# Weight-form stores on GpSimd's queue, and attention of batches 2 and 3 at other steps

## The chip, the cores and the metric

The kernel runs on one core of one Trainium2 chip. The metric is the device time of one execution in microseconds (us). TensorE (PE) multiplies and transposes, ScalarE (ACT) and VectorE (DVE) work element by element and empty TensorE's accumulator banks, GpSimd (POOL) and SyncE (SP) issue data transfers; ScalarE and VectorE issue none here.

## What is computed

Attention between tokens and a small state, then two feed-forward blocks one after the other. Sizes: x is 4 batches x 8 heads x 512 tokens x 64, the state 4 x 8 x 32 x 64; both blocks take 2176 rows (4 x 512 of x and 4 x 32 of the state) of width 512, with an inner width of 2048.

```python
def _attn_ref(x, state):
    scores = scale * np.matmul(x, state.transpose(0, 1, 3, 2))      # softmax over the state
    xread = np.matmul(softmax(scores), state)
    scores2 = scale * np.matmul(state, x.transpose(0, 1, 3, 2))     # softmax over the tokens
    sread = np.matmul(softmax(scores2), x)
    return np.concatenate([xread, sread], axis=2)
def _moe_ref(x, w_in, w_out):
    h = x @ w_in
    return (h - np.tanh(h)) @ w_out
def _moe2_ref(x, w_in, w_out):
    h = x @ w_in
    return (h * np.tanh(softplus(h))) @ w_out
def reference(...):
    return _moe2_ref(_moe_ref(tokens of _attn_ref, w1i, w1o), w2i, w2o)
```

## The kernel before, in words

**Precision and weights.** The inputs' weights are 64-bit floats, read as pairs of 32-bit words. `conv_steps` makes a 32-bit float of each: ScalarE makes `w` and `r` from the two words of a stage buffer (`st`, or one of three tiles `wide`), VectorE joins them, and ScalarE's reading of the buffer lets `load_next` issue the next 512 KB load (lines L187 and L189) into it. Matmuls are three products each (`mm3p`): every operand is split into a large part (`wh`, `gh`, `ath`, `swh`, `yh`: a ScalarE copy) and a small one (`wl`, `gl`, `atl`, `swl`, `yl`: a VectorE subtraction).

**Two phases.** Phase 1 is attention and the first block; phase 2 is the second block, with seven products (`m1` to `m7`) where eight would be needed. In phase 1 a loop runs over `seq`: 16 steps for each of batches 0, 1 and 2, four for the state rows, 16 for batch 3 (`start` is 0, 16, 32, 48 and 52; the phase ends at 68). A step multiplies up (`up_x`: `h<-ath,swh`, where `sw` is `state @ w_in`, made by `sw` in groups of side products `swp` for each quarter of the inner width), applies `h - tanh(h)` (`t`, `gh`, `gl`), and three steps later multiplies down into four accumulators (`acc`, banks a0 to a3). At the end of a batch the accumulators are evicted to `y`, those of the state steps (bank a0 alone) to `ys`. The next batch's `acc` matmuls need these banks.

**Side work.** Two more banks, s0 and s1, serve all small products in turn (`side_bank`): `swp` takes both, then come `xtp` (x transposed), `sct` (scores), `sc` and `e2p` (transposed back), `srd` (the state's read) and `atp`. Each must be evicted before the one after the next can use its bank. `side` holds what runs at which step, written by `at`. With `back=1` the work is held behind marks of the step before on each engine; with `narrow` the mark on TensorE alone.

**Background pieces.** While phase 1 runs, `keep_pace` runs pieces of the conversion of the second block's weights: convert, add, split, store. `store_split` and `steps_2o` put the two halves of a form into `stores`; `send` issues those that are old enough, 256 KB each (line L257), to DRAM (`wi` and `wo`), and frees the slot in SBUF of a form when HOLD = 6 more pieces have run. 96 such stores are issued. Phase 2 loads the forms again (`ws`, L793; `wo`, L800). A slot that is used again by another tile must wait until the store that reads it has landed; the wait stands on the engine that writes the tile.

Every engine runs its instructions in one order that is fixed when the program is built, and so does each queue: an issue that waits holds back those behind it. SyncE issues all loads of weights, all stores and the reloads; GpSimd issues the eight loads of x for batches 2 and 3.

Of the kernel before, what the change touches and what calls it, by code (L numbers as in the profile page):

```python
# [25 lines left out]
MOST = 3  # L26
# [46 lines left out]
def attention_moe_kernel(  # L73
# [10 lines left out]
    nc = tc.nc  # L84
# [16 lines left out]
    TE, AC, V = (Pinned(e, order) for e in (nc.tensor, nc.scalar, nc.vector))  # L101
# [19 lines left out]
    def put(*units):  # L121
        for u in units:
            if u.slot is None:
                halves.append(u)
            else:
                free.append(u.slot)
# [119 lines left out]
    def run_piece():  # L246


        bg.popleft()()
        now[0] += 1  # L250
        send(now[0] - 1, now[0] - HOLD)

    def send(ready, gone):
        while stores and stores[0][0] < ready:
            _, u, d = stores.popleft()
            v = u.t.bitcast(F32)
            nc.sync.dma_start(  # L257
                out=d, in_=v if len(d.shape) == 2 else v.rearrange("p (g e) -> p g e", g=2)
            )
            sent.append((now[0], u))  # L260
        while sent and sent[0][0] < gone:
            put(sent.popleft()[1])
# [128 lines left out]
    def at_xt(b, k):  # L391
        xt_t(b, k)
        xt_c(b, k)
# [31 lines left out]
    def at_scores(b):  # L425
        sc_m(b)
        for j in range(2):
            sc_c(b, j)
# [26 lines left out]
    def at_exp(b, j):  # L455
        sc_t(b, j)
        sc_max(b, j)
        sc_sub(b, j)
        sc_exp(b, j)
# [19 lines left out]
    def at_norm(b, j):  # L479
        nm_sum(b, j)  # L480
        nm_rec(b, j)
        nm_mul(b, j)
# [54 lines left out]
    def at_steps(b):  # L537
        st = [lambda k=k: at_xt(b, k) for k in range(KD - 1)]
        return st + [
            lambda: at_xt(b, KD - 1),  # L540
            lambda: at_scores(b),
            lambda: (at_exp(b, 0), at_exp_t(b, 0)),
            lambda: at_norm(b, 0),
            lambda: (at_exp(b, 1), at_exp_t(b, 1), at_read_t(b, 0)),
            lambda: at_norm(b, 1),
            lambda: at_read_t(b, 1),
            lambda: at_sread(b),
        ]
# [454 lines left out]
    engines = (TE, AC, V)  # L1003
    marks = []

    def at(step, fn, back=None, narrow=False):

        def held():
            kept = [e.floor for e in engines]
            for e, m in zip(engines, marks[-back]):  # L1010
                if e is TE or not narrow:
                    e.floor = m
            fn()
            for e, m in zip(engines, kept):
                e.floor = m

        side.setdefault(step, []).append(held if back else fn)

    seq = []
    start = {}  # L1020
# [24 lines left out]
                at(k + 3, lambda b=b: at_sread(b), 1)  # L1045
    for b in (2, 3):
        at(start[b - 1], lambda b=b: load_x(b))
        for i, f in enumerate(at_steps(b)):
            at(start[b - 1] + 3 + i, f, 1, True)
    for b in (1, 2, 3):  # L1050
        at(start[b] - (3 if b > 1 else 1), lambda b=b: at_a(b))
    at(start[3], lambda: bg.extend(pieces_y(0) + list(late)))
# [3 lines left out]
    def keep_pace(i):  # L1056
        for (s0, n0), (s1, n1) in zip(pace, pace[1:]):
            if s0 <= i < s1:
                goal = n0 + (n1 - n0) * (i + 1 - s0) / (s1 - s0)
                ran = done[0]  # L1060
                for _ in range(MOST):
                    if done[0] < goal and bg and len(free) >= RESERVE:
                        run_piece()
                        done[0] += 1
                if ran == done[0]:
                    now[0] += 3
                    send(now[0], now[0] - HOLD)
# [120 lines left out]
    AC.last = pre  # L1188
    background(len(bg), 0)
    send(now[0] + 1, 0)  # L1190
    bg.extend(tail)
    for f in loads_in(0):
# [54 lines left out]
```

## Time and profile before

| what | value |
|---|---|
| time, median of 3 runs | 736.38 us (735.43 to 737.16) |
| the profiled execution | 737.36 us, of which 735.2 is the span from the first to the last instruction |
| TensorE busy | 711.4 us, 97% of the span |
| VectorE, ScalarE, GpSimd busy | 466.7, 353.3 and 6.6 us |
| SyncE's queue (hardware) | 115.89 MB |
| GpSimd's queue (software) | 2.10 MB |
| TensorE's granted clock, mean | 0.991 of full speed |

Busy times are of one execution under the profiler and lie between its first and last instruction; about 2 us are outside them. A matmul of the usual form (128x128 by 128x512) follows the one before at 0.227 us, so twelve take 2.72 us in the chain of work. The granted clock is a share of 2.4 GHz; 0.5 is the lower level, 1.2 GHz.

### The profile page before, as it was taken

Reading aid. Unit: us, or ns where it says so; the run is one execution under the profiler, and the core shown is the slowest. Engines: PE = TensorE matmul, PEld = TensorE weight load, DVE = VectorE, ACT = ScalarE, POOL = GpSimd, SP = SyncE. Lnnn points to the kernel's source line nnn. Section 1 sums busy time; section 2 is a strip of 40 time slices with the busy share of each in tenths; the row PEclk is TensorE's granted clock in tenths of the full one; section 3 lists DMA queues with packets and bytes.
Section 4 is the critical chain, followed back from the end, with each engine's and each line's share of the span. In section 5 each row is a group of like instructions: output and inputs, shape, how many; then the busy total and the mean of one; then the engine's idle time right before and its main releaser. Section 6 shows DMA issues by size and latency. Waiting matters only on the chain.

```text
span 735.2 us, 10518 instructions
## 1 busy us (share of the span) xinstructions
PE 711.4 (97%) x3968; PEld 568.2 (77%) x3968; DVE 466.7 (63%) x791; ACT 353.3 (48%) x631; POOL 6.6 (1%) x14
## 2 busy tenths in 40 slices
PE   8899999999899999699999999999999999999997
PEld 6467877788677898477877888888788888888886
DVE  5899654866657658766836776555753465445554
ACT  6998544565755567655636442333333333222320
POOL 0000010000000000000000000000000000000000
PEclk9999999999999999889999999999999999999999
DMA  9984120036842569600997725554676343422003
GB/s 298 339 296 141 58 57 1 1 115 209 289 132 88 201 203 292 247 3 6 313 363 259 257 90 185 172 173 128 235 238 224 119 157 115 150 94 71 1 1 129
DMA packets 66978, 118.65 MB, mean 161 GB/s; under 512 B 7280, under 2 KB 28016, under 8 KB 66928
## 3 DMA queue, kind: packets, MB, share of 16 engines
q1 hardware_dynamic: 66288, 115.89, 48.0%
q0 software_dynamic: 640, 2.10, 0.9%
q8 instruction: 31, 0.51, 0.3%
q14 instruction: 19, 0.16, 0.1%
HBM read 88.34 MB, written 29.62 MB: 160 GB/s over the span
## 4 chain that ended last, share of the span: by engine, by line
PE 77%; ACT 10%; DVE 5%; DMA 5%; issue 1%; SPq 1%; DVEq 0%; ACTq 0%
PE acc L60 42%; PE h L60 28%; ACT w L60 2%; DMA wi<-wh 2%; ACT r L60 2%; PE hs L60 2%; PE swp L60 1%; DVE wide L60 1%; ACT gh L60 1%; DVE gl L60 1%; PE srd L60 1%; ACT wide L60 1%; ACT wh L60 1%; DMA x<-in_x_dram 1%; ACT swh L60 1%
## 5 line engine op out<-in xcount | busy, mean ns | idle before, releaser
L60 PE MATMUL acc<-wo,gh 128*128 128x512 f32 x544 | 167.9, 390 | 0.3 <-ACT gh L60 0.3
L60 PE MATMUL h<-yh,ws 128*128 128x512 f32 x448 | 157.0, 392 | 1.8 <-DVE wide L60 1.8
L60 PEld LDWEIGHTS acc<-wo,gh 128*128 128x128 f32 x544 | 101.5, 188 | 21.5 <-ACT gh L60 0.8
L60 PE MATMUL acc<-gh,wh 128*128 128x512 f32 x244 | 100.9, 413 | 8.5 <-ACT ys L60 6.3
L60 PE MATMUL acc<-wo,gl 128*128 128x512 f32 x272 | 106.0, 390 | 0.0
L60 PEld LDWEIGHTS h<-yh,ws 128*128 128x128 f32 x448 | 84.1, 188 | 20.8 <-DVE wide L60 3.6
L60 DVE TENSOR_TENSOR wide<-acc,wide 128x512 f32<-128x512 f32 (+1 forms) x85 | 57.9, 683 | 63.0 <-PE acc L60 61.4
L60 PE MATMUL acc<-gh,wl 128*128 128x512 f32 x244 | 96.8, 397 | 0.0
L60 PE MATMUL acc<-gl,wh 128*128 128x512 f32 x244 | 96.8, 397 | 0.0
L60 DVE TENSOR_TENSOR wide<-h,wide 128x512 f32<-128x512 f32 x97 | 66.6, 687 | 33.4 <-ACT wide L60 18.2
L60 PE MATMUL h<-yl,ws 128*128 128x512 f32 x224 | 87.3, 390 | 0.0
L60 DVE TENSOR_TENSOR gl<-wide,gh 128x512 fp32r<-128x512 f32 x74 | 51.1, 690 | 39.7 <-ACT gh L60 38.1
L60 ACT ACTIVATE wide<-wide 128x512 f32<-128x512 f32 x47 | 29.7, 633 | 79.5 <-DVE wide L60 79.5
L60 PEld LDWEIGHTS acc<-gh,wh 128*128 128x128 f32 x244 | 46.7, 192 | 26.7 <-ACT ys L60 6.7
L60 ACT ACTIVATE wide<-h 128x512 f32<-128x512 f32 x43 | 25.5, 593 | 81.2 <-PE h L60 81.1
L60 PEld LDWEIGHTS acc<-wo,gl 128*128 128x128 f32 x272 | 51.1, 188 | 11.0 <-DVE gl L60 0.4
L60 PEld LDWEIGHTS acc<-gh,wl 128*128 128x128 f32 x244 | 46.7, 191 | 10.3
L60 PEld LDWEIGHTS acc<-gl,wh 128*128 128x128 f32 x244 | 46.9, 192 | 9.3 <-issue 0.8
L60 PE MATMUL h<-ath,swh 128*128 128x512 f32 x128 | 51.7, 404 | 1.8 <-DVE t L60 1.6
L60 ACT ACTIVATE gh<-wide 128x512 fp32r<-128x512 f32 x74 | 46.7, 632 | 11.1 <-DVE wide L60 9.3
L60 PE MATMUL h<-atl,swh 128*128 128x512 f32 x128 | 50.2, 392 | 0.0
L60 PE MATMUL h<-ath,swl 128*128 128x512 f32 x128 | 50.1, 391 | 0.2 <-DVE swl L60 0.2
(156 smaller groups left out, 957.8 us busy)
## 6 DMA issues: line engine op xcount, KB each, us to landing
ws<-wi SPq DMA_DIRECT2D x128, 256.0 KB, 3.8
wo<-wo SPq DMA_DIRECT2D x64, 256.0 KB, 3.7
st<-in_moe_w_in_dram SPq DMA_DIRECT2D x27, 512.0 KB, 5.5
st<-in_moe_w_out_dram SPq DMA_DIRECT2D x22, 512.0 KB, 5.0
wi<-wh SPq DMA_DIRECT2D x32, 256.0 KB, 4.0
wi<-wl SPq DMA_DIRECT2D x32, 256.0 KB, 4.0
wide<-in_moe_w_out_dram SPq DMA_DIRECT2D x10, 512.0 KB, 5.2
wo<-wh SPq DMA_DIRECT2D x16, 256.0 KB, 3.8
```

Source lines behind the costliest of these rows:

```text
L60: i = fn(*args, **kw)
```

## The change

Three parts. (1) `send` issues the stores of weight forms on GpSimd's queue in place of SyncE's. (2) The eleven steps of attention of batches 2 and 3 stand at other distances from the batch's start, 3, 4, 5, 7 and so on to 15 in place of 3 to 13, and TensorE's part of them is no longer held behind the mark of the step before; the groups of `state @ w_in` stand at distances 2, 6, 10 and 14. (3) From step 58 on, `keep_pace` may run four pieces in a step in place of three. No instruction of TensorE, ScalarE or VectorE is added or taken away.

```diff
--- before.py
+++ after.py
@@ -254,7 +254,7 @@
         while stores and stores[0][0] < ready:
             _, u, d = stores.popleft()
             v = u.t.bitcast(F32)
-            nc.sync.dma_start(
+            nc.gpsimd.dma_start(
                 out=d, in_=v if len(d.shape) == 2 else v.rearrange("p (g e) -> p g e", g=2)
             )
             sent.append((now[0], u))
@@ -1003,13 +1003,12 @@
     engines = (TE, AC, V)
     marks = []
 
-    def at(step, fn, back=None, narrow=False):
+    def at(step, fn, back=None):
 
         def held():
             kept = [e.floor for e in engines]
             for e, m in zip(engines, marks[-back]):
-                if e is TE or not narrow:
-                    e.floor = m
+                e.floor = m
             fn()
             for e, m in zip(engines, kept):
                 e.floor = m
@@ -1045,8 +1044,8 @@
                 at(k + 3, lambda b=b: at_sread(b), 1)
     for b in (2, 3):
         at(start[b - 1], lambda b=b: load_x(b))
-        for i, f in enumerate(at_steps(b)):
-            at(start[b - 1] + 3 + i, f, 1, True)
+        for i, f in zip((3, 4, 5, 7, 8, 9, 10, 11, 12, 13, 15), at_steps(b), strict=True):
+            at(start[b - 1] + i, f)
     for b in (1, 2, 3):
         at(start[b] - (3 if b > 1 else 1), lambda b=b: at_a(b))
     at(start[3], lambda: bg.extend(pieces_y(0) + list(late)))
@@ -1058,7 +1057,7 @@
             if s0 <= i < s1:
                 goal = n0 + (n1 - n0) * (i + 1 - s0) / (s1 - s0)
                 ran = done[0]
-                for _ in range(MOST):
+                for _ in range(MOST + (i >= start[3] + 6)):
                     if done[0] < goal and bg and len(free) >= RESERVE:
                         run_piece()
                         done[0] += 1
```

The order of the program shows what moves. The first place is ScalarE's queue ahead of `ys`, the eviction of the state's accumulator; `t` and `gh` belong to the main path, `swh` to the next side products, `w`, `r`, `wh` and `yh` to the background pieces, and a wait on DMAHW or DMASW is one for a transfer of SyncE's or GpSimd's queue. Before:

```order
L60 ACTIVATE wh_3294<-w_3239 128x512 [waits PE_49]
L60 ACTIVATE yh_3512<-y_2190 128x512 [waits DMAHW4_49]
L60 ACTIVATE t_3255<-h_3248 128x512 [waits PE_49]
L60 ACTIVATE w_3341<-st_2925 128x512 [waits DMAHW3_49,PE_49]
L60 ACTIVATE swh_3276<-swp_3263 128x512 [waits DMAHW5_49,PE_49]
L60 ACTIVATE r_3342<-st_2925 128x512
L60 ACTIVATE gh_3258<-t_3255 128x512 [waits DMAHW1_49,DVE_49]
L60 ACTIVATE swh_3272<-swp_3262 128x512 [waits PE_49]
L60 ACTIVATE yh_3552<-yt_3354 128x512 [waits DMAHW1_49]
L60 ACTIVATE wh_3350<-w_3341 128x512 [waits DVE_49,PE_49]
L60 ACTIVATE ys_3292<-acc0_3126 128x512 [waits PE_49]
```

After:

```order
L60 ACTIVATE t_3166<-h_3159 128x512 [waits DMASW7_49,DMASW0_49,PE_49]
L60 ACTIVATE gh_3169<-t_3166 128x512 [waits DVE_49]
L60 ACTIVATE wh_3253<-w_3185 128x512 [waits PE_49]
L60 ACTIVATE r_3306<-st_2946 128x512 [waits DMAHW6_49,DVE_49]
L60 ACTIVATE t_3214<-h_3207 128x512 [waits PE_49]
L60 ACTIVATE wh_3299<-s34_3202 128x512 [waits PE_49]
L60 ACTIVATE swh_3235<-swp_3222 128x512 [waits PE_49]
L60 ACTIVATE gh_3217<-t_3214 128x512 [waits DVE_49]
L60 ACTIVATE swh_3231<-swp_3221 128x512 [waits DMASW6_49,PE_49]
L60 ACTIVATE yh_3470<-wide_73 128x512 [waits DMASW4_49]
L60 ACTIVATE ys_3251<-acc0_3085 128x512 [waits PE_49]
```

Of the ten items ahead of `ys` five waited for a transfer before (the two `yh`, `w`, a `swh` and `gh`) and four do after; behind the state's last `gh`, three items stood ahead of `ys`, and now two do.

The second place is SyncE's queue at the end of batch 1: loads (`st`) and stores (`wi`, `wo`) of weight forms. Before:

```order
L189 DMA st_2002<-in_moe2_w_in_dram 128x1024 [waits DMAHW0_49,Activation_49]
L189 DMA st_2010<-in_moe2_w_in_dram 128x1024 [waits DMAHW1_49,Activation_49]
L189 DMA st_2102<-in_moe2_w_in_dram 128x1024 [waits DMAHW3_49,DMAHW2_49,Activation_49]
L257 DMA wi_86<-wh_2092 128x2x256
L257 DMA wi_86<-wl_2093 128x2x256 [waits DMAHW4_49,DVE_49]
L257 DMA wo_111<-wh_2133 128x512 [waits DMAHW5_49]
L257 DMA wo_111<-wl_2134 128x512 [waits DMAHW6_49,DVE_49]
L257 DMA wo_112<-wh_2146 128x512 [waits DMAHW7_49]
L257 DMA wo_112<-wl_2147 128x512 [waits DMAHW0_49,DVE_49]
L189 DMA st_2141<-in_moe2_w_in_dram 128x1024 [waits DMAHW1_49,Activation_49]
```

After, SyncE's queue and GpSimd's at the same place:

```order
L189 DMA st_2029<-in_moe2_w_in_dram 128x1024 [waits DMAHW7_49,Activation_49]
L189 DMA st_2037<-in_moe2_w_in_dram 128x1024 [waits DMAHW1_49,Activation_49]
L189 DMA st_2129<-in_moe2_w_in_dram 128x1024 [waits DMAHW0_49,Activation_49]
L189 DMA st_2228<-in_moe2_w_in_dram 128x1024 [waits DMAHW2_49,Activation_49]
L189 DMA st_2272<-in_moe2_w_out_dram 128x1024 [waits DMAHW3_49,Activation_49]
```

```order
L257 DMA wi_86<-wh_2121 128x2x256 [waits DMASW6_49,Activation_49]
L257 DMA wi_86<-wl_2122 128x2x256 [waits DMASW7_49,DVE_49]
L257 DMA wo_111<-wh_2221 128x512 [waits DMASW0_49,Activation_49]
L257 DMA wo_111<-wl_2222 128x512 [waits DMASW1_49,DVE_49]
L257 DMA wo_112<-wh_2233 128x512 [waits DMASW2_49,Activation_49]
L257 DMA wo_112<-wl_2234 128x512 [waits DMASW3_49,DVE_49]
L257 DMA wo_113<-wh_2277 128x512 [waits DMASW4_49,Activation_49]
L257 DMA wo_113<-wl_2278 128x512 [waits DMASW5_49,DVE_49]
```

The loads now follow one another with no store between, and the stores stand behind stores.

The third place is ScalarE's queue ahead of `y`, the eviction of batch 1's accumulators. Before:

```order
L60 ACTIVATE t_2157<-h_2150 128x512 [waits PE_49]
L60 ACTIVATE swh_2178<-swp_2165 128x512 [waits DMASW3_49,PE_49]
L60 ACTIVATE gh_2160<-t_2157 128x512 [waits DVE_49]
L60 ACTIVATE swh_2174<-swp_2164 128x512 [waits PE_49]
L60 ACTIVATE w_2307<-st_2010 128x512 [waits DMAHW3_49,DMAHW1_49]
L60 ACTIVATE y_2185<-acc0_1307 128x512 [waits PE_49]
L60 ACTIVATE r_2308<-st_2010 128x512 [waits DMAHW4_49]
L60 ACTIVATE y_2195<-acc2_1309 128x512 [waits PE_49]
```

After:

```order
L60 ACTIVATE wide_72<-h_2134 128x512 [waits PE_49,Activation_49]
L60 ACTIVATE swh_2161<-swp_2148 128x512 [waits DMASW0_49,PE_49]
L60 ACTIVATE gh_2143<-wide_72 128x512 [waits DVE_49]
L60 ACTIVATE swh_2157<-swp_2147 128x512 [waits PE_49]
L60 ACTIVATE w_2281<-st_1747 128x512 [waits DMAHW1_49,DMASW0_49]
L60 ACTIVATE wide_72<-acc0_1307 128x512 [waits DVE_49,PE_49]
L60 ACTIVATE y_2177<-acc2_1309 128x512 [waits PE_49]
```

The first eviction of an accumulator stood behind a `w` that waits for two transfers of SyncE's queue; it now stands behind a `w` that waits for one of each queue. (The tile of the first eviction has another name because a slot of `wide` serves it.)

The fourth place is TensorE's queue behind the side products for batch 2's second group. Before, one transpose follows the last `swp` behind nine `acc` matmuls:

```order
L60 MATMUL swp_2361<-w_545,sbt_76 32x512
L60 MATMUL acc0_2225<-gh_2214,wh_541 128x512
L60 MATMUL acc0_2225<-gl_2215,wh_541 128x512
L60 MATMUL acc0_2225<-gh_2214,wl_542 128x512
L60 MATMUL acc1_2226<-gh_2214,wh_541 128x512
L60 MATMUL acc1_2226<-gl_2215,wh_541 128x512
L60 MATMUL acc1_2226<-gh_2214,wl_542 128x512
L60 MATMUL acc2_2227<-gh_2214,wh_541 128x512
L60 MATMUL acc2_2227<-gl_2215,wh_541 128x512
L60 MATMUL acc2_2227<-gh_2214,wl_542 128x512
L60 MATMUL xtp_2379<-ident_75,x_2072 128x128 [waits DMASW4_49,DVE_49]
```

After, it stands behind all twelve and the six of `h`:

```order
L60 MATMUL acc2_2207<-gh_2194,wl_542 128x512
L60 MATMUL acc3_2208<-gh_2194,wh_541 128x512
L60 MATMUL acc3_2208<-gl_2195,wh_541 128x512
L60 MATMUL acc3_2208<-gh_2194,wl_542 128x512
L60 MATMUL h_2373<-ath_1860,swh_2157 128x512 [waits DVE_49]
L60 MATMUL h_2373<-atl_1862,swh_2157 128x512
L60 MATMUL h_2373<-ath_1860,swl_2158 128x512
L60 MATMUL h_2373<-ath_1869,swh_2161 128x512
L60 MATMUL h_2373<-atl_1871,swh_2161 128x512
L60 MATMUL h_2373<-ath_1869,swl_2162 128x512
L60 MATMUL xtp_2387<-ident_75,x_2060 128x128 [waits DMASW6_49,DVE_49]
```

The transposes moved nine matmuls further from the group whose banks they use.

## Rows read from the trace of the kernel before

**Rows 1.** The page, busy time, share and instructions of each engine
```profile
PE 711.4 (97%) x3968; PEld 568.2 (77%) x3968; DVE 466.7 (63%) x791; ACT 353.3 (48%) x631; POOL 6.6 (1%) x14
```

**Rows 2.** What TensorE waited for: releaser, us in total, times, longest
```profile
PE acc L60 <- ACT ys L60: 6.3, 1, 6.3
...
PE acc L60 <- ACT y L60: 2.2, 1, 2.2
```

**Rows 3.** The chain of work, 300 to 319 us: start, us, what
```profile
310.43 5.49 PE acc L60 x12
315.92 1.78 PE h L60 x6
```

**Rows 4.** Timeline of TensorE, 300 to 320: start, us, instruction, idle before
```profile
310.43 0.80 PE L60 MATMUL acc<-gh,wh 128*128 128x512 f32 x1 [6.28 <-ACT ys L60]
```

**Rows 5.** Timeline of ScalarE, 296 to 312 us
```profile
305.14 0.63 ACT L60 ACTIVATE yh<-y 128x512 fp32r<-128x512 f32 x1 [2.05 <-DMA wo<-wh]
...
309.77 0.60 ACT L60 ACTIVATE ys<-acc 128x512 f32<-128x512 f32 x1
```

**Rows 6.** Stretches: us, busy time of each engine, granted clock, DMA share, GB/s
```profile
180.00:200.00 20.00, 17.27 (x83) 12.87 (x82) 13.71 (x23) 14.36 (x27) 1.44 (x2) 0.93 0.91 307
...
303.50:318.00 14.50, 8.22 (x26) 6.18 (x25) 10.51 (x17) 7.76 (x15) 0.00 (x0) 0.65 0.45 165
```

**Rows 7.** The chain of work, 196 to 206 us
```profile
190.35 6.09 DMA wi<-wh
...
197.73 4.35 PE acc L60 x12
```

**Rows 8.** Timeline of SyncE's queue, 181 to 197 us
```profile
186.05 4.26 SPq L189 DMA_DIRECT2D st<-in_moe_w_in_dram  x3
```

**Rows 9.** The chain of work, 206 to 240 us
```profile
220.04 2.95 PE acc L60 x12
...
228.91 2.72 PE acc L60 x12
231.63 1.36 PE h L60 x6
```

**Rows 10.** The stores' line: durations ns min/median/max, first and last start, waits, landing
```profile
L257 SPq DMA_DIRECT2D wi<-wh x32: 359/374/1419, 160.0 to 367.5; - x32
...
L257 SPq DMA_DIRECT2D wo<-wl x16: 319/320/1180, 192.0 to 411.2; - x16
...
  ACT yh L60: 4.7, 2
  ACT w L60: 4.6, 2
...
DMA to landing us min/median/max: 2.1/3.9/6.5
```

**Rows 11.** The loads' line: issues on GpSimd, duration ns min/median/max, first and last start
```profile
L363 POOL DMA_DIRECT2D x<-in_x_dram x6: 722/722/838, 90.8 to 164.9; - x6
```

**Rows 12.** The page, DMA issues: count, KB each, median us to landing
```profile
st<-in_moe_w_out_dram SPq DMA_DIRECT2D x22, 512.0 KB, 5.0
...
x<-in_x_dram POOLq DMA_DIRECT2D x6, 256.0 KB, 3.2
...
wide<-in_x_dram POOLq DMA_DIRECT2D x2, 256.0 KB, 5.5
```

**Rows 13.** Timeline of TensorE, transposes that waited, 190 to 240 us
```profile
194.83 0.66 PE L60 MATMUL xtp<-ident,wide 128*128 128x128 f32 x4 [0.48 <-DVE swl L60]
...
216.28 0.66 PE L60 MATMUL xtp<-ident,x 128*128 128x128 f32 x4 [0.39 <-DVE swl L60]
...
235.53 0.65 PE L60 MATMUL e2p<-ident,scs 128*128 128x128 f32 x4 [0.63 <-DVE swl L60]
```

**Rows 14.** Timeline of ScalarE, 255 to 297 us
```profile
282.78 0.60 ACT L60 ACTIVATE wide<-acc 128x512 f32<-128x512 f32 x1
```

**Rows 15.** Timeline of TensorE, 281 to 290 us
```profile
286.31 0.48 PE L60 MATMUL acc<-wh,gh 128*128 128x512 f32 x1
```


## The prediction

> **What bounds the kernel now.** I read the page first. TensorE is busy for nearly the whole span [rows 1], so the kernel is bound by TensorE and only its own gaps and slow stretches can be won back; VectorE's and ScalarE's idle time is worth nothing by itself. Second came the list of what TensorE waited for. One wait stands far above the rest, for `ys`, the eviction of the finished state accumulator, and the next that this change can touch is that for `y`, the eviction of batch 1 [rows 2]. Then I followed both through the chain of work and ScalarE's timeline.
>
> The state wait: TensorE stands still for 6.28 us and goes on at 310.43 [rows 4]. ScalarE is free before that, but stands 2.05 us in front of a split `yh` whose slot is freed by the landing of a `wo` store, and then has nine items queued ahead of `ys`, which starts at 309.77 [rows 5]. The granted clock of the stretch that holds this gap is 0.65, a mix of the two levels, 2.4 and 1.2 GHz [rows 6]. So the twelve `acc` matmuls behind the wait take 5.49 us and the six `h` matmuls 1.78 us [rows 3], where twelve and six take 2.72 and 1.36 elsewhere [rows 9].
>
> The `y` wait: SyncE's queue holds loads and stores in one order. At 186.05 three loads take it 4.26 us [rows 8], the store behind them is issued at 190.35 and lands 6.09 us later, and only then may ScalarE write a `w` that stands ahead of `y` [rows 7]. The twelve matmuls behind take 4.35 us [rows 7], where behind a set of small side products they take 2.95 [rows 9].
>
> In all, ScalarE waited for landings of stores in four places, 4.7 us at `yh` and 4.6 us at `w` [rows 10].
>
> **Part 1, stores on GpSimd's queue.** 96 issues leave SyncE; GpSimd, which has 8 loads, gets them. GpSimd computes nothing in this stretch. An issue on SyncE took 0.374 us in the middle [rows 10], one on GpSimd 0.722 [rows 11], so 96 issues are about 69 us of an engine that idles: no cost by itself. What changes is the order: a store no longer stands behind a load that waits for a stage buffer, and no load stands behind a store. Landing on SyncE's queue was 2.1 to 6.5 us, 3.9 in the middle [rows 10]; GpSimd's loads of the same size took 3.2 and, in the crowded stretch, 5.5 [rows 12].
>
> *The state wait.* After the change one item with a store ahead of it is left before `ys`, a `yh`, and its store (`wi_96<-wl_3254`) has its data 2.9 to 4.5 us before the state accumulator is done, an estimate from the matmuls that lie between in the order, at the pace of rows 9. From there: issue 0.72, landing 3.2 or 5.5, so 3.9 or 6.2 us; then two ScalarE items of about 0.5 us; and six `h` matmuls (1.36 us) that TensorE still has. With 3.2 the stall is 0 to 0.7 us, with 5.5 it is 1.4 to 3.0. Traffic there is light (165 GB/s against 307 in the transition, [rows 6]), so I take the quiet landing and 0.3 us. Gain: 6.28 for the wait, 5.49 - 2.72 = 2.77 and 1.78 - 1.36 = 0.42 for the clock, 9.47 us; left over, 0.3.
>
> *The transition from batch 1 to 2.* The stores leave the loads' queue, and no store behind loads holds the `w` ahead of `y` any more; a 512 KB load may. That load is issued only when the buffer has been read, six ScalarE items earlier, about one step of TensorE (12 + 6 matmuls, 4.08 us, [rows 9]) and its side products; a load of this size lands in 5.0 us [rows 12]. Gain: 2.2 for `y` [rows 2], 0.48 at the transposes just before [rows 13], which came late for the same backlog, and 4.35 - 2.95 = 1.40 for the clock: 4.1 us. I leave 0.3 (bounds 0 and 1.7, the latter if the load lands 1.4 us later than that).
>
> **Part 2, attention of batches 2 and 3 at other steps.** Nothing is added or removed; the transposes go where no group of `state @ w_in` products has just taken both side banks. Two waits behind such a group go: at 216.28 (0.39) and 235.53 (0.63) [rows 13], since at the first the next transposes stand 18 matmuls behind the group and no longer 9: 1.02 us. Two waits of the same kind further ahead, in batch 1, stay: there a transpose still stands within some nine matmuls of the group. Four new places appear, where a product or transpose follows the one before it by only 0 to 2 matmuls and needs a bank that ScalarE or VectorE must first evict. No row shows these; the nearest are the waits just named, 0.39 to 0.63 each, and none has a second eviction ahead of it as those had, so 0 to 0.45 each; I take 0.9 for the four (bounds 0 and 2.5).
>
> **Part 3, four pieces in place of three from step 58.** Conversions run a little earlier near the end of the phase. After the state stretch TensorE has slack in front of every reload of forms, and the order of MoE2 is as before, so I take nothing. Its cost, if the cover is gone, would be ScalarE items ahead of `h` evictions, 0.5 us each.
>
> **A cost that the new order brings.** Between batch 2 and the state steps ScalarE must evict accumulator 0 before the state sums start. Before, that ran at 282.78 [rows 14], some 0.6 us long, and TensorE wanted it at 286.31 [rows 15]: 2.9 us to spare. After, four conversions in a row stand ahead of it, each needing a 512 KB load that is issued only when the buffer before it is read. Worked through with load landings of 4 to 5.5 us (5.0 in the middle, [rows 12]), ScalarE comes out 0 to 3 us late. I take 1.0, near the lower end because the loads no longer stand behind stores.
>
> **Sum.** Gains 9.47 + 4.1 + 1.02 = 14.6; costs 0.3 + 0.3 + 0.9 + 1.0 = 2.5; net -12.1 us. The profiled execution took 737.36, 0.98 above the median shown, 736.38. So 725.3 for such an execution, **724.3** as a median. 0.2% is 1.5 us, about what a measurement of this kernel can tell from no change.
>
> **Rivals.**
> - *A: the wait comes back in another place.* `yh` before `ys` waits for a store that lands in 5.5 us, or the load chain ahead of accumulator 0 is 3 us late, and the clock falls again. For: GpSimd's two crowded loads took 5.5 [rows 12], and 2.2 us of standing still were followed by slow matmuls [rows 7]. Against: the state stretch is quiet. Price: 2.7 us more of stall and 3.2 of clock (2.77 + 0.42): 730.2; with one of the two alone 727 to 730, with both places hit 733.5 (2.0 more of stall and 1.3 of clock).
> - *B: the queue changes nothing but who issues.* Landing, not order, made the waits: 6.09 us of landing against 4.26 in SyncE's queue [rows 7, 8]. Then both big stalls stay, part 2 gives 1.0 - 0.9, and the time is 735 to 738, 736.3 in the middle. Against: `w` could have been written 4 us earlier with the store issued on time, and nine items no longer stand ahead of `ys`. The Trainium skill (DMA: Bandwidth & Descriptors, "Issuing engines are not separate DMA queues") says that transfers of all issuing engines share the same 16 DMA engines and that issuing from several saves only issue time. By that rule 736.3; the trace shows 4.26 us of such issue time at 186.05 [rows 8], more than the rule calls usual.
> - *C: slower, GpSimd's queue becomes the bound.* Stores ran from 160.0 to 411.2 us [rows 10], 96 of them, 2.6 us apart on average. If an issue on GpSimd took longer than that, the queue would fall behind, slots would come free late, and the splits that need them, then `ys` and the reloads, would wait. MoE2's reloads have some 14 us of slack (an estimate from the order, at the pace of rows 9), so the forecast's 12 us are gone when the lag is 26 us, at 2.9 us an issue (0.27 x 96); at 3.0 us it lags 38, and the time is 724.3 + 38 - 14 = 748. Against: all 6 loads of the row took 0.72 to 0.84 [rows 11], and two more 0.72 while VectorE was busy 13.7 of 20 us [rows 6]. The Trainium skill (SBUF — State Buffer, "A bandwidth-pool intuition that's wrong (but worth ruling out)") states that a transfer issued by GpSimd takes about 620 ns alone and about 3100 beside a VectorE copy, since its descriptors can't be written meanwhile. By that figure the lag is 48 us and the time 758; the eight loads here don't show it.
>
> **How the numbers follow.** Chances: forecast (721 to 727) 0.60, A 0.24, B 0.06, C 0.10. Lower end: costs at their lower bounds, 724.3 - 2.5 = 721.8, and 1 us of spread between runs, so 720.8. Upper end: A with both places hit, 733.5. That leaves out B, C and little else, under 2 in 10. The likeliest case's own range is 721 to 727.5. Faster by over 0.2%: forecast and A, 0.84. Within 0.2%: B, 0.06. Slower: C, 0.10.
>
> **What will show it.** Right: no TensorE wait for `ys` over 1 us; the granted clock at 1.0 from 196 to 206 and from 290 to 305 (the stretch moves forward by some 5 us); GpSimd with 104 issues of 0.7 us; SyncE's loads issued without a store between; waits for e2p, xtp, sct, atp of about 0.5 us each in number, not in size. Wrong: an `acc` wait of 2 us or more at the state sums with `yh` or `w` ahead of it, or clock below 0.9 there; an issue on GpSimd of over 2 us; `ws` reloads that TensorE waits for. The step I trust least is the landing of stores from GpSimd, since the trace has loads from there only.

## The result and the profile after

| | before | changed |
|---|---|---|
| median, 4 runs each, us | 736.77 (735.43 to 738.65; the three of the first table and one more) | **728.22** (726.63 to 729.65) |
| ratio | | 0.9882, 95% [0.985, 0.9913] |
| profiled execution, us (span) | 737.36 (735.2) | 726.63 (724.9) |

Changed is faster by 8.5 us in the median and by 10.7 us between the two profiled executions. The profiled execution of the changed kernel was its fastest, and the only one of the four with a mean granted clock of 1.000 (the others 0.995 to 0.998); that matters below.

The page of the changed kernel first: the row of the engines, then three rows of DMA issues (count, KB each, median us from issue to landing). They answer to [rows 1] and [rows 12].

```profile
PE 708.0 (98%) x3968; PEld 566.0 (78%) x3968; DVE 464.3 (64%) x791; ACT 352.9 (49%) x631; POOL 70.4 (10%) x110
...
st<-in_moe_w_in_dram SPq DMA_DIRECT2D x27, 512.0 KB, 5.9
...
wi<-wh POOLq DMA_DIRECT2D x32, 256.0 KB, 4.5
...
wo<-wh POOLq DMA_DIRECT2D x16, 256.0 KB, 5.4
```

TensorE has the same 3968 matmuls. GpSimd's busy time is now that of issuing, and the stores did not land in the 3.2 us of the quiet `x` loads.

What TensorE waited for (us in total, times, longest), against [rows 2]:

```profile
PE acc L60 <- ACT ys L60: 1.7, 1, 1.7
...
PE acc L60 <- ACT wide L60: 0.4, 1, 0.4
PE e2p L60 <- DVE swl L60: 0.4, 1, 0.4
```

The `ys` wait went from 6.3 to 1.7, the wait for `y` (whose first eviction is now named `wide`) from 2.2 to 0.4, and the side banks cost 0.4 at the dearest of the new places. The chain of waits at the state sums (start, duration), against [rows 3]:

```profile
299.15 2.82 DMA wi<-wl
301.99 0.03 ACT yh L60
...
302.53 0.59 ACT ys L60
...
303.16 3.06 PE acc L60 x12
306.22 1.36 PE h L60 x6
```

A `yh` waits for a store of `wl` to land, `ys` follows, and TensorE goes on at 303.16. This is the one item that the prediction said would be left ahead of `ys`. Here the clock held, and the twelve and six matmuls took 3.06 and 1.36 us, against 5.49 and 1.78. The windows show the clock (last three columns: granted clock, DMA share, GB/s):

```profile
180.00:200.00 20.00, 19.58 (x100) 15.06 (x99) 14.12 (x25) 13.47 (x25) 8.36 (x12) 1.00 0.69 237
...
300.00:312.00 12.00, 10.35 (x48) 8.20 (x47) 10.64 (x18) 9.87 (x19) 5.33 (x9) 1.00 0.82 256
```

Both are at 1.00, where [rows 6] had 0.93 and 0.65. The DMA engines are not quiet at the state sums any more: 256 GB/s, where the window of [rows 6] that holds the gap moved 165. While the store above was under way, from 299.15 to 301.97 us, the rate was 232.

**Where the time came from.** From step 21 on, every step of the main path but the state's four has six `h` matmuls, and the start of the first of them marks the step in TensorE's timeline. The mark of step 36, the first behind the eviction of `y`, stood at 201.91 before and stands at 199.54 now; that of step 57 stood at 320.75 and stands at 310.63. Differences between such marks split the gain by stretch (us, changed less before, profiled executions; "stores alone" and "steps alone" are the first two experiments):

| stretch | forecast | changed | stores alone | steps alone |
|---|---|---|---|---|
| start to step 21 | 0 | +0.7 | +2.2 | +1.6 |
| 21 to 35 (new side-bank waits) | +0.9 | +0.8 | 0.0 | +0.7 |
| 35 to 36 (transition, `y`) | -3.8 | **-3.8** | **+3.8** | -4.6 |
| 36 to 48 (old side-bank waits) | -1.0 | -0.3 | 0.0 | -1.3 |
| 48 to 55 (batch 2 to the state) | +1.0 | 0.0 | +1.8 | 0.0 |
| 55 to 57 (state sums, `ys`) | -9.2 | **-7.5** | -1.3 | **-8.7** |

The first line lies before the first store (156.3 us); over all the kernels run here it lies between -0.2 and +3.3 us, and nothing is read from it. In the fourth line a new wait of TensorE stands beside the old ones that went, for `xt` (x transposed, evicted by ScalarE) at about 211 us: 0.4 us in the changed kernel, none in e2, but 1.0 and 1.8 us in two other runs with the same steps (e12 and e6 below). The two places of the forecast gave the gain, in nearly the forecast sizes. Which part of the change gave it is another matter.

### The profile page after: what moved, and what is told of

Same layout as the page of the kernel before. It is cut to its first block, busy times and chain, and to the rows that moved or that the text cites. A ratio compares the mean times of both kernels' runs of the same rounds, so it can differ in the third digit from the quotient of the medians.

```text
span 724.9 us, 10570 instructions
## 1 busy us (share of the span) xinstructions
PE 708.0 (98%) x3968; PEld 566.0 (78%) x3968; DVE 464.3 (64%) x791; ACT 352.9 (49%) x631; POOL 70.4 (10%) x110
## 4 chain that ended last, share of the span: by engine, by line
PE 72%; issue 12%; ACT 6%; POOL 4%; DVE 4%; DMA 1%; SPq 0%; POOLq 0%; DVEq 0%; ACTq 0%
PE acc L60 39%; PE h L60 26%; POOL wi L257 3%; ACT w L60 2%; ACT r L60 2%; PE hs L60 2%; PE swp L60 1%; POOL wo L257 1%; PE srd L60 1%; DMA x<-in_x_dram 1%; DVE gl L60 1%; ACT gh L60 1%; DVE wide L60 1%; ACT t L60 1%; ACT swh L60 1%
## 5 line engine op out<-in xcount | busy, mean ns | idle before, releaser
L60 PE MATMUL acc<-gh,wh 128*128 128x512 f32 x244 | 99.3, 407 | 2.1 <-ACT ys L60 1.7
```

Of the source, the lines that this page charges most:

```text
L60: i = fn(*args, **kw)
```

## The experiments

**1 and 2: each part alone.** e1 has only the queue changed, e2 only the steps and pieces (stores on SyncE, as before).

```diff
 # e1_stores_only, in send
-            nc.sync.dma_start(
+            nc.gpsimd.dma_start(
 # e2_steps_only, where the steps are placed (and the at() and keep_pace of the change)
-        for i, f in enumerate(at_steps(b)):
-            at(start[b - 1] + 3 + i, f, 1, True)
+        for i, f in zip((3, 4, 5, 7, 8, 9, 10, 11, 12, 13, 15), at_steps(b), strict=True):
+            at(start[b - 1] + i, f)
```

> Part 1 alone: stores of weight forms on GpSimd's queue, attention steps and pieces per step as before. My account (the stores' place in SyncE's queue made the transition's wait, and the item order on ScalarE the state wait): the transition's gain of 3.8 us comes here, the state wait does not, since the store that held it was issued at once and landed in 2.5 us; TensorE's wait for ys stays at 5 to 7 us, and the time is 732.5 to 734. Rival (the queue makes both gains): wait for ys below 2.5 us and 726 to 729. Rival (the queue gives nothing): both waits as before, 735.5 to 737.5.

> Parts 2 and 3 alone: new attention steps and four pieces from step 58, stores on SyncE's queue as before. My account: the order on ScalarE ahead of ys is nearly that of the full change, so most of the state gain of 7.5 us comes, and the y wait of the transition stays at 2 us or more: 729 to 732. Rival (the queue makes both gains): the wait for ys stays above 4 us and the time is 735 to 738.

Measured: e1 741.65 us, ratio 1.0071 [1.0047, 1.0095]: **slower**, by 4.8 us against the 736.89 of the kernel before run beside it. e2 724.52, ratio 0.9847 [0.982, 0.9875]: faster by 12.4. Both lie outside every range that was written down for them. All that was gained came from the steps, and the queue, to which the prediction gave 13.6 of its 14.6 us of gains, costs time. TensorE's waits in e1:

```profile
PE xtp L60 <- DVE swl L60: 7.0, 3, 6.1
PE acc L60 <- ACT ys L60: 5.0, 1, 5.0
```

`ys` is 5.0 us late on GpSimd's queue too, and the transition is worse than before. ScalarE's timeline shows why (start, duration; in brackets idle time before it and what ended that):

```profile
189.57 1.21 ACT L60 ACTIVATE w<-st 128x512 f32<-128x512 f32 x2 [1.59 <-DMA wi<-wh]
...
194.59 0.66 ACT L60 ACTIVATE r<-st 128x512 uint32<-128x512 uint32 x1 [1.70 <-DMA st<-in_moe_w_in_dram]
...
198.03 0.66 ACT L60 ACTIVATE w<-st 128x512 f32<-128x512 f32 x1 [2.26 <-DMA st<-in_moe_w_in_dram]
198.60 0.64 ACT L60 ACTIVATE r<-st 128x512 uint32<-128x512 uint32 x1
199.14 0.58 ACT L60 ACTIVATE t<-h 128x512 f32<-128x512 f32 x1
199.62 0.59 ACT L60 ACTIVATE swh<-swp 128x512 fp32r<-128x512 f32 x1
```

A store wait is still there (1.59), and two conversions then wait 1.70 and 2.26 us for 512 KB loads, with `t` and `swh` of the main path queued behind them. That place in the queue is new too: in the kernel before, the same `w` stands behind `t` and both `swh`, right ahead of `y` (third place of the change section). So the edit of the queue alone also changed ScalarE's order here, and the 4.8 us hold both. The loads were not freed by the removal of the stores from their queue: SyncE's timeline has four of them spread over 12 us, although each is issued in 0.33, since in the program's order each waits for the ScalarE item that reads its buffer free.

```profile
187.48 12.12 SPq L189 DMA_DIRECT2D st<-in_moe_w_in_dram  x4
```

The store that held this `w` before did go out sooner. It is the `wi<-wh` that SyncE issued at 190.35 and that landed at 196.44 [rows 7]; in e1 GpSimd issues it at 185.38, and it lands after 6.1 us again, at 191.49:

```profile
185.38 0.73 POOL L257 DMA_DIRECT2D wi<-wh  x1
```

But the load of the same `w`, there at 192.15 before, now came at 197.95. The three loads of this place landed in 4.8 to 5.8 us before and in 7.0 to 9.3 in e1 (line L189, us from issue to landing, least, middle and most; before, from 186 to 192 us, then e1, from 187 to 193):

```profile
DMA to landing us min/median/max: 4.8/5.0/5.8
```

```profile
DMA to landing us min/median/max: 7.0/7.1/9.3
```

And the stretch is full. The window of e1 has the DMA engines busy 0.97 of it, and the stores issued from 176 to 196 us landed in 6.6 us in the middle (6.1 before):

```profile
180.00:200.00 20.00, 16.53 (x84) 12.42 (x82) 11.90 (x22) 13.01 (x24) 10.13 (x16) 1.00 0.97 336
...
DMA to landing us min/median/max: 4.1/6.6/8.1
```

In e2 nothing is wrong at the state sums: `yh` has no idle time ahead of it, and TensorE waits 0.5 us for `ys`.

```profile
298.87 0.63 ACT L60 ACTIVATE gh<-t 128x512 fp32r<-128x512 f32 x1
299.39 0.60 ACT L60 ACTIVATE swh<-swp 128x512 fp32r<-128x512 f32 x1
299.86 0.65 ACT L60 ACTIVATE yh<-wide 128x512 fp32r<-128x512 f32 x1
300.39 0.60 ACT L60 ACTIVATE ys<-acc 128x512 f32<-128x512 f32 x1
```

**3: which of the two parts that move no DMA.** e6 takes the fourth piece out of e2, and e3 takes it out of the changed kernel:

```diff
-                for _ in range(MOST + (i >= start[3] + 6)):
+                for _ in range(MOST):
```

> Part 2 alone: new attention steps, stores on SyncE's queue, three pieces in a step to the end. If part 3 is worth nothing, as forecast: 724 to 725.5, as parts 2 and 3 together (724.5). Rival (the fourth piece matters once the stores are on SyncE's queue, since five fewer pieces are done when phase 1 ends): 726 to 728, with waits of TensorE behind 350 us.

> The changed kernel without part 3: three pieces in a step to the end. My account, that part 3 is worth nothing: 727.5 to 729, as the changed kernel. Rival (the fourth piece brings the end of phase 1 forward or delays evictions): 1 us or more off in either direction, with new waits of TensorE between 310 and 360 us.

Measured: e6 725.37, ratio 0.9844 [0.9819, 0.987]; e3 727.1, ratio 0.9879 [0.9849, 0.9909]. They stand where e2 and the changed kernel stand, so the fourth piece is worth nothing that can be measured, and part 2 alone is worth some 12 us.

**4: which batch's steps.** The new distances for one of the two batches, the other at 3 to 13, stores on SyncE (e9 batch 2, e10 batch 3):

```diff
+        new = (3, 4, 5, 7, 8, 9, 10, 11, 12, 13, 15) if b == 2 else range(3, 14)
+        for i, f in zip(new, at_steps(b), strict=True):
+            at(start[b - 1] + i, f)
```

> New attention steps for batch 2 alone (batch 3 at the old distances), four pieces from step 58, stores on SyncE's queue. The two batches' steps lie in different stretches (16 to 31 and 32 to 47), so I expect their gains apart: batch 2's takes the y wait of the transition away (wait for y or for the first eviction there below 0.6 us), worth about 4.5 us; the state wait depends on which pieces have run by then, here 3 to 4 fewer than before at step 55 in place of 7, so it should stay at 2 us or more: 730 to 734. Rival (batch 2's steps alone shift all pieces behind them enough): both waits gone, 724 to 727.

> New attention steps for batch 3 alone, four pieces from step 58, stores on SyncE's queue. ScalarE's order ahead of ys is here that of the kernel with pieces left out in steps 45 and 46, which still waited 4.8 us for ys: wait for ys 3.5 to 6 us, the y wait of the transition 2 us or more as before, 735 to 738.5. Rival (moving batch 3's attention itself makes the state gain): wait for ys below 2 us, 728 to 731.

Measured: e9 733.75, ratio 0.9948 [0.9929, 0.9966]; e10 737.7, ratio 0.9997 [0.9981, 1.0013]. TensorE's timeline in e9, at the state sums, where the eviction of `ys` is named `wide`, as its slot is of that pool:

```profile
307.56 0.80 PE L60 MATMUL acc<-gh,wh 128*128 128x512 f32 x1 [5.01 <-ACT wide L60]
```

Batch 2's steps mend the transition (steps 35 to 36: -4.4 us) and leave most of the state's wait. What they change there shows in the window from 180 to 200 us, in e9 and in e10:

```profile
180.00:200.00 20.00, 20.00 (x102) 15.49 (x101) 14.00 (x24) 13.50 (x25) 1.45 (x2) 1.00 0.71 237
```

```profile
180.00:200.00 20.00, 17.46 (x88) 13.15 (x87) 14.06 (x25) 14.65 (x28) 1.44 (x2) 0.98 0.93 312
```

All kernels with the old distances of batch 2 move 307 to 336 GB/s in this stretch (before [rows 6], e1, e5, e10) and wait there 2.2 us or more for `y` or a transpose; all with the new ones, here and below, move 231 to 242 and wait 1.1 us at most. TensorE's waits in e10 show that batch 3's alone mend neither:

```profile
PE acc L60 <- ACT ys L60: 4.1, 1, 4.1
...
PE acc L60 <- ACT y L60: 2.5, 1, 2.5
```

-3.7 and 0 do not add up to -12. At the state (steps 55 to 57) the profiled executions gain 2.2 us in e9 and 3.5 in e10, against 8.7 with both: most of the gain there needs both batches' new distances.

**5: is it only that fewer pieces run?** The new distances keep slots longer, so in the program's order 36 background pieces are through by the end of step 47 (43 before), and 60 by the end of step 55 (67 before). e5 is the kernel before with the same fourth piece and two steps in which no piece may run, which leaves 62 by step 55:

```diff
-                for _ in range(MOST):
+                for _ in range(0 if i in (45, 46) else MOST + (i >= start[3] + 6)):
```

> The kernel before with one edit in the pace of background pieces: none in steps 45 and 46, and four in place of three from step 58 to catch up. Attention steps and the stores' queue are those of before. New account: the new attention steps hold more slots, so fewer pieces fit in (33 done by step 46 in place of 40), and the splits yh of the next phase's input, which come after piece 66 and wait for a slot, no longer stand ahead of ys. Then this edit alone takes most of the state wait away (6.28 us and the clock behind it): wait for ys below 2 us, 727.5 to 731, with the y wait of the transition as before. Rival (the place of the attention work itself, or its release from the marks, made the gain): wait for ys above 4 us, 735 to 738.

Measured: 738.43, ratio 1.0009 [0.9991, 1.0027]. The account by number of pieces falls. In ScalarE's timeline another reused slot has taken the place of the old one:

```profile
293.77 0.66 ACT L60 ACTIVATE w<-st 128x512 f32<-128x512 f32 x1 [4.21 <-DMA wi<-wh]
```

One `w` waits 4.21 us for a store, and `ys` is 4.8 us late in this run. e10, with 62 pieces as well, has the same kind of wait. That points to which items stand ahead of `ys`, and which of them reuse a slot whose store has just been issued, rather than to how many pieces have run. e9 does not fit it: there no item of ScalarE's near the state waits for a store. The last long wait is for a load, at 293.30, and from 300.68 to `ys` ScalarE works through twelve items without a pause:

```profile
293.30 0.66 ACT L60 ACTIVATE r<-st 128x512 uint32<-128x512 uint32 x1 [2.86 <-DMA st<-in_moe_w_out_dram]
```

So a late store is one way to a late `ys`, and an unbroken run of conversions is another.

**6: `ys` on the other engine.** VectorE evicts the state in place of ScalarE, in the changed kernel (e4) and in e2 (e8):

```diff
-            evac(u.t, ACC["s"], 0)
+            evac(u.t, ACC["s"], 1)
```

> The changed kernel with one edit: the eviction of the state accumulator to ys runs on VectorE in place of ScalarE. My account: the 1.7 us that the changed kernel still waits for ys is ScalarE standing in front of a yh until a store from GpSimd has landed, and in executions where that takes longer the clock falls too; with ys elsewhere both go: wait for ys under 0.7 us, granted clock 1.000 in all runs, 725 to 726.5 and less spread. Rival (VectorE's queue is as late there as ScalarE's): the wait stays at 1.5 us or more and the time at 727.5 to 729.5.

> Parts 2 and 3, stores on SyncE's queue, and the eviction to ys on VectorE: an attempt at a better version. With part 1 the same edit left 1.5 us of wait, now for ys on VectorE; if what was late there was VectorE's queue behind late ScalarE work, the 0.5 us that parts 2 and 3 still wait for ys stays within 0.3 of that: 724 to 725.5. If VectorE is free there, the wait goes and the time is 723.5 to 724.

Measured: e4 727.19, ratio 0.9868 [0.9841, 0.9895]; e8 727.31, ratio 0.986 [0.9834, 0.9886]. Neither is better than without the edit, and e8 lies outside both of its ranges. In e4 `ys` no longer stands behind the `yh`, and TensorE waits for it all the same:

```profile
PE acc L60 <- DVE ys L60: 1.5, 1, 1.5
```

VectorE has five operations in a row there, `ys` the last. The late `yh` is not alone there: with `ys` moved out from behind it, TensorE's wait is 0.1 us shorter than in the changed kernel (1.52 and 1.65), and no more. In e8 TensorE stands still for 2.34 us at the same place. The profile puts that down to an `r` on ScalarE, which ended 0.05 us later than `ys`; but `ys` on VectorE ended at 305.48, and TensorE went on 0.15 us behind it, the same distance as in e4. So VectorE's queue was the later one: TensorE waited 1.9 us longer than in e2.

**7: the other way to part loads and stores.** e2, with the loads of MoE2's weights on GpSimd and the stores left on SyncE:

```diff
-            nc.sync.dma_start(out=t, in_=src)
+            (nc.gpsimd if key[0][:2] == "w2" else nc.sync).dma_start(out=t, in_=src)
```

> Parts 2 and 3 with the loads of the second block's weights on GpSimd's queue, the stores on SyncE's. Stores and loads are in two queues again, but the stores are issued by SyncE. Account A (what part 1 costs is that GpSimd issues a store later and that each issue takes longer): no store is late, 724 to 725.5. Account B (the cost comes from stores and loads in two queues running at the same time, so that each lands later): 727 to 729. Account C (a load issued by GpSimd is as late as a store was): a wait for w or r of a 512 KB load ahead of y at 190 to 200 us, over 729.

Measured: 731.88, ratio 0.993 [0.9909, 0.9951], 6.5 us over e6, the same steps run beside it. This is the time and the wait of account C. The load ahead of `y` was late, by ScalarE's timeline:

```profile
197.53 0.66 ACT L60 ACTIVATE w<-st 128x512 f32<-128x512 f32 x1 [2.58 <-DMA st<-in_moe_w_out_dram]
```

The stores, alone on SyncE's queue among the weight forms, were no faster for it, by the DMA rows of its page (4.8 and 4.7 us in e2):

```profile
wi<-wh SPq DMA_DIRECT2D x32, 256.0 KB, 5.3
wi<-wl SPq DMA_DIRECT2D x32, 256.0 KB, 5.6
```

The load ahead of `y` is the smallest part of the loss: by the marks, e7 is behind e2 by 1.4 us from step 35 to 36, by 3.2 from 36 to 48 and by 3.5 from 55 to 57. Whichever of the two is parted from the other, the kernel loses.

**8: the changed kernel, and with its stores back on SyncE, side by side.** The only difference is the line of e1, and here ScalarE's and TensorE's order is the same in both, so this pair prices the queue by itself.

> The changed kernel as it is, timed beside the next one on one chip to measure part 1 directly: 727 to 729 (0.986 to 0.990 of the kernel before).

> The changed kernel with its stores on SyncE's queue, beside the one above. If part 1 costs what the traces show (0.7 us at the transition, 1.2 at the state wait, some 0.5 between, and the clock where the state wait is long): 2 to 4 us less than the run above, 724 to 725.5. If the difference seen before was chance: within 1 us of it.

Measured: e11 728.78, ratio 0.9873 [0.9852, 0.9894], five runs from 726.6 to 729.28; e12 725.05, ratio 0.9829 [0.9807, 0.9852], four runs from 724.28 to 726.71. On the same chip the queue costs 3.7 us with the new steps (4.8 with the old ones in e1, where ScalarE's order moved as well). **e12, which is e2 over again, beats both kernels.** The chain of e11 at the state sums, and the window there:

```profile
299.84 2.81 DMA wi<-wl
...
303.21 0.59 ACT ys L60
...
303.84 4.24 PE acc L60 x12
308.08 1.76 PE h L60 x6
```

```profile
300.00:312.00 12.00, 9.87 (x39) 7.66 (x38) 9.69 (x17) 9.63 (x19) 5.11 (x9) 0.86 0.80 258
```

The same `yh`, the same store, a wait of 2.1 us in place of 1.7, and here the clock fell. The twelve and six matmuls took 1.58 us more than in the first profile (4.24 + 1.76 less 3.06 + 1.36). The marks of the profiled executions of e11 and e12 split the difference: e11 is behind by 0.7 us from step 35 to 36, ahead by 0.4 from 36 to 48, and behind by 3.3 from 55 to 57.

**Where the queue's cost lies.** One store decides at the state sums, that of `wi_96`, with two halves `wh` and `wl`. In the changed kernel ScalarE writes `wh` and then an `r`, and GpSimd issues (two timelines):

```profile
296.00 0.61 ACT L60 ACTIVATE wh<-w 128x512 fp32r<-128x512 f32 x1
297.45 0.67 ACT L60 ACTIVATE r<-st 128x512 uint32<-128x512 uint32 x1 [0.84 <-DVE wl L60]
```

```profile
298.42 0.73 POOL L257 DMA_DIRECT2D wi<-wh  x1 [3.17 <-ACT r L60]
299.15 0.72 POOL L257 DMA_DIRECT2D wi<-wl  x1
```

`wh` was complete at 296.61, and GpSimd had been idle for 3.17 us when it issued the store at 298.42. By the profile the `r` behind `wh` let it go, 0.30 us after that `r` ended (298.12), although in the program this store waits for `wh` alone. `wl`, ready at 297.42 (VectorE's timeline: 296.73 + 0.69), went out behind it at 299.15 and landed at 301.97. In e2 `wh` is complete at 295.98, and SyncE's queue has:

```profile
296.01 0.36 SPq L257 DMA_DIRECT2D wi<-wh  x1
296.82 0.36 SPq L257 DMA_DIRECT2D wi<-wl  x1
```

Each goes out 0.03 us after its data. From `wl` written to `wl` issued it is 1.73 us on GpSimd and 0.03 on SyncE, and in the changed kernel TensorE waited 1.65 us. At the transition the queue's cost is a load: the 512 KB that the `w` ahead of `y` needs took 5.50 us to land beside GpSimd's stores (189.86 to 195.37) and 4.07 in e2 (190.69 to 194.75); in the pair e11 and e12 it took 5.55 and 4.97.

## Why the prediction was right, and where it was not

**Time and direction: right.** 724.3 (720.8 to 733.5) against 728.22; -12.1 us against -10.7 between the two profiled executions and -8.5 in the medians. The bound, the two stalls and their prices in clock were read rightly: the transition gave 3.8 of 3.8 us net, the state 7.5 of 9.2, and MoE2 nothing. But that the time fell into the range was luck: 13.6 us of the forecast's gains were put down to part 1, which costs time, and the gain came from part 2, which the forecast held to be worth 0.1 net of its costs.

**Part 1, "What changes is the order: a store no longer stands behind a load": this step failed.** It is a true statement of the order, and worth less than nothing in time. With the queue alone (e1) both stalls stay. The store that held the `w` ahead of `y` went out 5.0 us sooner and landed 5.0 us sooner, as the step says; but the load of the same `w` landed 5.8 us later (2.2 of it from the first stretch of the table), and a `w` needs both. The prediction let that load land in 5.0 us in a stretch in which the DMA engines were busy 0.91 of the time [rows 6]; with the stores beside the loads it took 7.1. As for its answer to rival B, one reading was wrong. The 4.26 us "taken" by three loads [rows 8] is a group of the timeline, with the waits between its issues in it; the line of the loads in the kernel before, from 180 to 205 us, says how long one is (ns, least, middle and most):

```profile
L189 SPq DMA_DIRECT2D st<-in_moe_w_in_dram x4: 328/338/346, 186.0 to 198.3; - x4
```

Three are 1 us of issuing, and the rest is waiting: by the order rows of the change section each load waits for a ScalarE item, and in e1 a queue of their own did not shorten that. Rival B, that landing and not order made the waits, was nearer for part 1 than the forecast, though too kind: it gave 0, and the runs +4.8 and +3.7. The rule of the Trainium skill that it quoted (DMA: Bandwidth & Descriptors, "Issuing engines are not separate DMA queues") leads the same way, that another issuer saves issue time and no more; the runs bear it out, and show a loss besides. The prediction held 4.26 us of issue time against that rule, which the row just shown takes back.

**Part 2, "1.02 us": it gave some 12, since its main effect was left out.** I priced the steps by TensorE's side-bank waits alone, and those came out near the forecast in the changed kernel and e2 (+0.8 for the new ones, -0.3 and -1.3 for the old, though +2.0 in e6, where the wait for `xt` stood). But other steps hold other slots, so `keep_pace` runs its pieces at other times, and another mix of conversions and splits stands ahead of `y` and `ys`. My rows of ScalarE's order showed that mix before and after, and I credited all of it to the queue. Shown: the gain follows the steps (e1, e2, e6), the transition's part needs batch 2's, most of the state's needs both (e9, e10), and fewer pieces ahead of the state alone do nothing (e5). The release of TensorE's part from the mark of the step before moved no instruction: placed with it and without it, the program's order is the same. The runs agree: in e10 batch 2, and in e9 batch 3, is released at its old distances, and the wait for `y` (2.5 us) and that for `ys` (5.0) are still there. At the transition the traffic goes with the gain (231 to 242 GB/s against 307 to 336), which no run separates from the order of the items. Argued only, for the state: that what decides is which of the items ahead of `ys` reuse a slot with a store under way. It fits the idle time ahead of a `w` in e5 and e10 and ahead of a `yh` in the changed kernel, but not the late `ys` of e9, and no run moved a single item. Why the state needs both batches' steps stays open.

**"Left over, 0.3" at the state sums: 1.65 to 2.1, and mostly with the clock** (the mean granted clock lay below 1.000 in eight of the nine executions of the changed kernel). I took a store from GpSimd as issued within 0.72 us of its data and landing in 3.2. Landing was kinder (2.82 us), but the issue came 1.7 us after the data. The quiet landing was also argued from a stretch that would not stay quiet, 165 GB/s before and 256 after. By the prediction's own signs this is where it fails: it asked for no wait for `ys` over 1 us, and e11 shows what it named as wrong, an `acc` wait of 2 us behind a `yh` and a clock below 0.9. This is rival A's place. In the execution of e11 the clock fell as well, and the median of 728.2 lies in A's 727 to 730 with one of its two places hit, 0.7 above the upper end of the forecast's own 721 to 727.5.

**The small costs.** Side-bank waits 0.9: measured 0.8 from step 21 to 35, and behind it the wait for `xt`, 0 to 1.8 us by run, which at its worst brings the sum to the bound of 2.5. Batch 2 to the state 1.0: measured 0; that forecast was too dear, and the loads there were in time. Part 3, nothing: nothing (e3, e6).

**Rival C: refuted.** GpSimd's issues in the changed kernel (ns, least, middle and most):

```profile
L257 POOL DMA_DIRECT2D wi<-wh x32: 715/725/735, 156.3 to 356.4; - x32
...
L257 POOL DMA_DIRECT2D wo<-wl x16: 540/540/555, 196.5 to 401.2; - x16
...
DMA to landing us min/median/max: 2.3/4.9/9.3
```

None of the 96 came near 2.9 us, with VectorE busy 64% of the span. The Trainium skill's figure of some 3100 ns beside a VectorE copy (SBUF — State Buffer, "A bandwidth-pool intuition that's wrong (but worth ruling out)") did not appear here: the longest issue of a `wi` form was 735 ns. Three of the issues, all of `wo` forms, ran beside a copy of VectorE's, and they took 540 ns like the others; those copies read an accumulator or side bank.

## What to carry to other kernels

A store that lands late behind a queue's loads was not mended here by another queue. Look first at what else the waiting instruction needs, at how long one issue takes (a row that groups several holds their waits too), at what else moves while the store is under way, and at how soon the issuing engine learns that its data are there. When a change moves steps of the main path and a pacing rule fills in background work by free slots, compare the whole order of the engine that waits, and price each part of the change with the other part undone; an order that holds both parts cannot say which of them made it. A stall of about 2 us on TensorE was followed by slow matmuls in some executions and not in others, so a forecast should carry that price (here 1.6 us) for any stall that it leaves.

## What the runs showed of the hardware that was not expected

- GpSimd went on 0.30 us after the instruction that released it had ended, SyncE's queue 0.03 us. In the changed kernel GpSimd stood idle until the data came ahead of 39 stores; 38 of them went out 0.29 to 0.30 us after their data. The 39th, that of `wi_96`, went out 1.8 us after its own, and so it did in e3, e4 and e11. By the profile the instruction behind held it; why stays open.
- An issue on GpSimd took 0.725 us in the middle for the `wi` forms and 0.540 for the `wo` forms, though both are of 256 KB; they differ in shape (two halves of 256 columns, one of 512).
- The queue hardly changed landing in the middle (3.9 us before and 4.1 in e1; 4.7 in e2 and 4.9 in the changed kernel), and the 512 KB loads of the two matrices show no steady effect of it over a whole run either: 5.9 and 5.5 us in the changed kernel and 5.5 and 4.7 in e2, but 5.1 and 4.9 in e1 and 5.5 and 5.0 before. What rose was single loads in a full stretch, as above.
- TensorE stood still for 1.65 us in one execution and the granted clock stayed at 1.00; 2.1 us in another of the same kernel, and the window shows 0.86, a mix of 2.4 and 1.2 GHz. After 2.34 us at the state sums the clock was 0.72 over the next 6 us in e7 and 1.00 in e8.
